# Second-pair sums of y kept in DRAM by accumulating transfers, in a fused attention and two-MLP kernel

## The chip, the cores and the metric

One core of one Trainium2 chip runs the whole program. The metric is device microseconds per execution. The kernel before takes 1046.27 us, the median of 3 runs (1044.96 to 1047.87).

## The reference

Everything is float32. Attention with a soft cap runs over 4 batch rows, 12 heads, 448 positions and head size 64; its result goes through two MLPs.

```
scores = cap * tanh(q @ k.T / sqrt(64) / cap);  x = softmax(scores) @ v     # (4, 12, 448, 64) -> (1792, 768)
h = x @ w_in;  g = h * cos(h);  y = g @ w_out                               # 768 -> 2048 -> 768
a = y @ w1;  b = y @ w2;  out = ((a * b) @ w3) @ w_out2                     # 768 -> 1024 -> 1024 -> 768
```

The w tensors reach the device in double-width words and are converted there. The first MLP's output y is what the change touches.

## The kernel before

**Layout.** Data lie transposed: a tile is 128 features by the 448 positions of one batch row, and the 768 features of y are six such tiles, numbered m = 0 to 5. A product of two float32 operands is three matmuls on high and low parts (`mm3`, L389 to L392), so every product shows as equal numbers of L390, L391 and L392.

**Stages.** Attention for all batch rows comes first, together with the product w3 @ w_out2 (`make_w34`). Then `moe1` makes y. Its first pair of batch rows (b = 0, 1) goes through plain products, unit by unit: a unit is 256 of the 2048 hidden features for one batch row, so a batch row has 8 units. For the second pair (b = 2, 3) both batch rows are worked together in 8 pair steps (`h_step`), each a seven-product scheme of Strassen and Winograd on quarter blocks; sums of x (tiles xS1, xS2, ...) and of w_in (tiles stx, ht, hb) are its operands. Then `moe2` does the second MLP, again by seven products per step, and reads y back from the DRAM scratch `y_d`: for the first pair around its start, for the second pair near its middle (`lefts(1, ...)`).

**y.** For each unit and each m, `y_part` runs six matmuls into a PSUM bank. The first unit of a batch row is copied from the bank to the SBUF tile `y` (ScalarE or VectorE). Each of the 7 later units is added to it by one VectorE instruction that reads bank and tile and writes the tile. After the last unit, SyncE sends the tile to `y_d`. The ring `y_r` has two slots of six tiles; the second MLP takes them over for its own sums (`low`, `high`, shown as y too: `y<-bank,w`, `y<-bank,hs`).

**Order of the work.** A planner in the program (`Plan.schedule`) makes the instruction order of each engine before anything runs. Each operation has a due time, which is a priority and not a start time, and one or more engine options with a cost. The planner is greedy: an engine that is free takes the ready operation that is due first, if ring slots are free. "AD" lets the planner choose ScalarE or VectorE, "PD" GpSimd or VectorE. It models a shared port: an operation that takes the port (all of GpSimd's, and VectorE's with a fourth field in the option) waits for another one that holds it. `pair_due` spaces the pair steps by `pd`; the due times of the second MLP follow from it. All DMAs of the kernel before are issued by SyncE, in planned order, and a DMA at the head of that queue that waits holds up those behind it.

**Pools.** SBUF pools open when others close. Pool lp (tiles rawl, stl) opens when hx closes (the last products of the pair steps), and q2 (tiles rawq, stq) when mp closes (the last y parts). The second MLP converts its weights w1 and w2 in the single slots of rawl and rawq: load, ScalarE L924, GpSimd L930, VectorE L937 and L941, then differences (stq) and high and low parts (xh, xl). The slot rawl first serves the loads of the left operands (A12, S1, S4).

A second copy of the program for caps above 40 sits behind a branch that these inputs don't take.

Of the kernel before, what the change touches and what calls it, by code (L numbers as in the profile page):

```python
# [15 lines left out]
ALU = mybir.AluOpType  # L16
# [4 lines left out]
B, H, S, D = 4, 12, 448, 64  # L21
# [10 lines left out]
BH = B // 2  # L32
# [105 lines left out]
class Plan:  # L138
# [57 lines left out]
    def schedule(self):  # L196
# [10 lines left out]
        free = dict(PE=1.0, ACT=2.0, DVE=3.4, POOL=1.5, SP=1.2, port=0.0)  # L207

        def port(x):
            return x[0] == "POOL" or len(x) > 3  # L210

        free[None] = 0.0
        table, order, t, line = "exp", [], 0.0, 0.0
# [6 lines left out]
        while done < len(self.ops):  # L220
# [6 lines left out]
            for c in cands:  # L227
                o = c[2]
                if o.table and table and o.table != table and o.due > t - SLACK_T and any(
                        x[2].table == table for x in cands):  # L230
                    rest.append(c)
                    continue
                pick = min(o.opts, key=lambda x: max(free[x[0]] - t, free["port"] - t if port(x) else 0.0, 0.0) + wait.get(x[0], 0.0) + x[1] * (PAR.get("w" + (x[0] or ""), 1.0) if o.due < PAR["tw"] else 1.0))
                if pick[0] in idle and port(pick) and free["port"] > t + 1e-9:
                    pick = None
                elif pick[0] not in idle:
                    if len(o.opts) == 1:
                        wait[pick[0]] = wait.get(pick[0], 0.0) + pick[1] * PAR["back"]
                    pick = None
# [9 lines left out]
                for it in o.allocs:  # L249
                    it.ring.queue.remove(it)  # L250
                    it.slot = heapq.heappop(it.ring.free)[1]
                (e, cost, f), two = pick[:3], port(pick)
                if o.table:
                    if table != o.table:
# [49 lines left out]
    ql=6, qs=3,  # L304
    hsw=27,
    wb=(20.0, 81.0), we=(81.5, 150.5), e1=2.6, e2=15.1, e3=20.0,
    m0=163.0, ua=14, pa=19.6, pu=14.75, pd=27.4,
    wlead=3.1,


# [7 lines left out]
    m0=222.0, ua=13, pa=19.15, pu=14.2, nt=9, nph=3,  # L318
# [22 lines left out]
def program(  # L341
# [15 lines left out]
    PE, ACT, DVE, POOL, SP = nc.tensor, nc.scalar, nc.vector, nc.gpsimd, nc.sync  # L357
    G = dict(PAR, **GENERAL) if general else PAR
    plan = Plan()
# [4 lines left out]
    def copy(due, dst, src, n, on, psum=False):  # L364
        opts = {
            "A": ("ACT", (0.051 if psum else 0.094) + n / 1200, lambda: ACT.copy(dst(), src())),  # L366
            "D": ("DVE", 0.068 + n / (960 if psum else 1920), lambda: DVE.tensor_copy(dst(), src()))  # L367
            + (() if psum else (True,)),
            "P": ("POOL", 0.16 + n / 1200,
                  lambda: POOL.tensor_scalar(dst(), src(), 1.0, 0.0, op0=ALU.mult, op1=ALU.add)),  # L370
        }
        plan.op(due, [opts[e] for e in on], r=[src], w=[dst])

    def tt(due, dst, a, b, n, op, on="D", psum=False):
        opts = {
            "D": ("DVE", 0.068 + n / 960, lambda: DVE.tensor_tensor(dst(), a(), b(), op=op))  # L376
            + (() if psum else (True,)),
            "P": ("POOL", 0.158 + n / 480, lambda: POOL.tensor_tensor(dst(), a(), b(), op=op)),  # L378
        }
        plan.op(due, [opts[e] for e in on], r=[a, b], w=[dst])  # L380
# [4 lines left out]
    def dma(due, dst, src, r=(), w=(), kb=115, write=False):  # L385
        plan.op(due, [("SP", 0.66, lambda: SP.dma_start(dst(), src()))], r=r, w=w,
                kb=kb)

    def mm3(out, wh, wl, xh, xl, first, last, on=False):  # L389
        PE.matmul(out, wh, xh, start=first, stop=False, skip_group_check=on)  # L390
        PE.matmul(out, wh, xl, start=False, stop=False, skip_group_check=on)  # L391
        PE.matmul(out, wl, xh, start=False, stop=last, skip_group_check=on)  # L392
# [60 lines left out]
    psum = pools["psum"].pool  # L453
# [24 lines left out]
    y_d = Scratch("dram", [B, KD, P, S], "y_d")  # L478
# [537 lines left out]
    def pair_due(n):  # L1016
        d = G["pd"]
        return unit_due(2 * NP) + (n - 0.26 * (n > 1)) * d

    def unit_due(u):  # L1020
        return G["m0"] + min(u, G["ua"]) * G["pa"] + max(u - G["ua"], 0) * G["pu"]
# [33 lines left out]
    def moe1(raw_r, x_r):  # L1055
# [14 lines left out]
        of = {b: [u for u, x in enumerate(units) if x[1] == b] for b in range(B)}  # L1070
# [58 lines left out]
        def y_part(u, m, due):  # L1129
            g, b = units[u]  # L1130
            gh, gl = g_t[u]
            if u == of[b][0] and m == 0:
                yacc[b] = y_r.new()
            acc = hy_r.ref()
            ws = [w_t["o", g, c] for c in range(2)]

            def f():
                for c in range(2):
                    mm3(acc()[:, :S], ws[c][0]()[:, m * P:(m + 1) * P], ws[c][1]()[:, m * P:(m + 1) * P],
                        gh()[:, c, :], gl()[:, c, :], c == 0, c == 1)  # L1140

            plan.op(due, [("PE", 6 * MM, f)], r=[gh, gl, *ws[0], *ws[1]], w=[acc])
            ya = yacc[b].at(m, lambda t: t[:, m, :])
            if u == of[b][0]:
                copy(due + 1, ya, acc[:, :S], S, "AD", psum=True)
            else:
                tt(due + 1, ya, acc[:, :S], ya, S, ALU.add, psum=True)
            if u == of[b][-1]:
                z = y_d.at((b, m), lambda d: d[b, m])
                dma(due + 3, z, ya, r=[ya], w=[z], kb=230, write=True)  # L1150

# [137 lines left out]
        for u, (g, b) in enumerate(units[:2 * NP]):  # L1289
            u0 = unit_due(u)  # L1290
            pu = unit_due(u + 1) - u0
            if b == groups[g][1][0]:
                weights(g, u0 - G["wlead"])
            for c in range(2):
                wi = w_t["i", g, c]
                hp = hy_r.ref()
                for kp in range(3):
                    due = u0 + (c * 3 + kp) * pu / 6
                    ks = (2 * kp, 2 * kp + 1)

                    plan.op(due, [("PE", 6 * MM, mm_h(hp, wi, ks, xh[b], xl[b]))],
                            r=[*wi, *(z.at(k) for k in ks for z in (xh[b], xl[b]))], w=[hp])
                    if u >= 2:
                        y_part(u - 2, 3 * c + kp, due + pu / 12)
                chain(u, c, hp[:, :S], u0 + (c + 1) * pu / 2)
        half = 36 * MM * 1.02

        def y_pair(n):
            u, after = 2 * NP + 2 * n, pair_due(n + 2) if n + 2 <= NP else pair_due(NP) + 2 * half
            for m in range(KD):  # L1310
                y_part(u, m, after - half + (m + 0.5) * half / KD)
            for m in range(KD * (n + 1 < NP)):
                y_part(u + 1, m, after + (m + 0.5) * half / KD)
# [3 lines left out]
        for n in range(NP):  # L1317
            u, u0, u1 = 2 * NP + 2 * n, pair_due(n), pair_due(n + 1)
# [296 lines left out]
```

## Time and profile before

| | |
|---|---|
| median of 3 runs | 1046.27 us |
| profiled execution | 1047.94 us, span 1046.1 us |
| TensorE (PE) busy | 1022.7 us, 98% |
| VectorE (DVE) busy | 917.8 us, 88% |
| ScalarE (ACT) busy | 566.5 us, 54% |
| GpSimd (POOL) busy | 242.7 us, 23% |
| DMA engines | 50.7% of the span, all from hardware queues |

Busy time is a mean over stages with different limits, so the stages are read one by one. A matmul shows as about 0.36 us but the next one starts 0.20 us after it; a busy share of 100% on PE therefore says little, and the number of matmuls in a window against its length divided by 0.20 us says more. SPq is SyncE's queue, which issues the DMAs. An idle time in brackets is the wait before that instruction and what ended it.

### The profile page before, as it was taken

Reading aid. Unit: us, or ns where it says so; the run is one execution under the profiler, and the core shown is the slowest. Engines: PE = TensorE matmul, PEld = TensorE weight load, DVE = VectorE, ACT = ScalarE, POOL = GpSimd, SP = SyncE. Lnnn points to the kernel's source line nnn. Section 1 sums busy time; section 2 is a strip of 40 time slices with the busy share of each in tenths; the row PEclk is TensorE's granted clock in tenths of the full one; section 3 lists DMA queues with packets and bytes.
Section 4 is the critical chain, followed back from the end, with each engine's and each line's share of the span. In section 5 each row is a group of like instructions: output and inputs, shape, how many; then the busy total and the mean of one; then the engine's idle time right before and its main releaser. Section 6 shows DMA issues by size and latency. Waiting matters only on the chain.

```text
span 1046.1 us, 15415 instructions
## 1 busy us (share of the span) xinstructions
PE 1022.7 (98%) x5560; PEld 872.6 (83%) x5560; DVE 917.8 (88%) x1388; ACT 566.5 (54%) x780; POOL 242.7 (23%) x191
## 2 busy tenths in 40 slices
PE   7999999989999999999999999999999999999997
PEld 2577777768888877897999999999888999999997
DVE  6899999989999999999999889899799888767642
ACT  6779777978687767635564333443334346212121
POOL 4353220212444231225103223211122100000000
PEclk9999999999999999999999999999999999999999
DMA  7666886766665545653545211228455557211132
GB/s 255 203 195 191 232 249 172 224 185 208 208 193 191 182 146 178 194 187 108 191 148 167 95 57 53 103 84 286 154 193 171 166 182 242 79 63 61 61 112 87
DMA packets 82839, 168.84 MB, mean 161 GB/s; under 512 B 19650, under 2 KB 55874, under 8 KB 82754
## 3 DMA queue, kind: packets, MB, share of 16 engines
q1 hardware_dynamic: 82754, 167.78, 50.7%
q8 instruction: 45, 0.74, 0.3%
q14 instruction: 40, 0.33, 0.1%
HBM read 128.94 MB, written 38.62 MB: 160 GB/s over the span
## 4 chain that ended last, share of the span: by engine, by line
PE 46%; DVE 5%; DMA 0%; issue 0%; POOL 0%; ACT 0%; SPq 0%; DVEq 0%; POOLq 0%; ACTq 0%
PE bank L390 16%; PE bank L392 15%; PE bank L391 15%; DVE xl L376 1%; DVE stl L937 1%; DVE y L376 1%; DVE stl L941 1%; DMA rawq<-in_w 0%; DVE stq L376 0%; DVE w34h L367 0%; DVE w34l L376 0%; DVE rawx L376 0%; DVE hs L376 0%; DVE wol L376 0%; DVE g L376 0%
## 5 line engine op out<-in xcount | busy, mean ns | idle before, releaser
L390 PE MATMUL bank<-g,woh 128*128 128x448 f32 x384 | 140.8, 367 | 2.8 <-DVE zs L367 2.8
L392 PE MATMUL bank<-g,wol 128*128 128x448 f32 x384 | 139.8, 364 | 0.0
L391 PE MATMUL bank<-g,woh 128*128 128x448 f32 x384 | 139.3, 363 | 0.0
L672 ACT ACTIVATE double<-double,ts 112x896 f32<-112x896 f32 x96 | 93.8, 982 | 28.9 <-PE double L658 20.3
L376 DVE TENSOR_TENSOR y<-bank,y 128x448 f32<-128x448 f32 x168 | 101.3, 614 | 8.3 <-PE bank L392 8.1
L390 PE MATMUL bank<-xh,wih 128*128 128x448 f32 x264 | 97.1, 368 | 1.9 <-ACT xh L366 1.3
L672 ACT ACTIVATE p<-double,pac 112x896 f32<-112x896 f32 x96 | 96.4, 1013 | 3.1 <-PE bank L706 1.8
L391 PE MATMUL bank<-xl,wih 128*128 128x448 f32 x264 | 96.2, 365 | 1.2 <-POOL xl L378 1.2
L392 PE MATMUL bank<-xh,wil 128*128 128x448 f32 x264 | 96.5, 365 | 0.0
L366 ACT COPY hs<-bank 128x448 f32<-128x448 f32 x72 | 38.2, 531 | 97.3 <-PE bank L392 97.3
L390 PEld LDWEIGHTS bank<-g,woh 128*128 128x128 f32 x384 | 72.3, 188 | 13.9 <-DVE zs L367 3.1
L701 PE MATMUL bank<-p,v 112*32 112x448 f32 x768 | 78.9, 550 | 0.0
L392 PEld LDWEIGHTS bank<-g,wol 128*128 128x128 f32 x384 | 72.5, 189 | 5.3
L391 PEld LDWEIGHTS bank<-g,woh 128*128 128x128 f32 x384 | 72.2, 188 | 4.8
L392 PE MATMUL bank<-ab,w34l 128*128 128x448 f32 x192 | 69.6, 363 | 0.6 <-DVE w34l L376 0.6
L390 PE MATMUL bank<-ab,w34h 128*128 128x448 f32 x192 | 69.7, 363 | 0.0
L391 PE MATMUL bank<-ab,w34h 128*128 128x448 f32 x192 | 69.3, 361 | 0.0
L376 DVE TENSOR_TENSOR p<-p 112x448 f32<-112x448 f32 x79 | 60.3, 765 | 2.5 <-ACT p L672 2.3
L930 POOL TENSOR_SCALAR wx<-rawc 128x768 f32<-128x768 f32 x29 | 39.8, 1373 | 95.1 <-ACT rawc L924 60.5
L701 PEld LDWEIGHTS bank<-p,v 112*32 112x32 f32 x768 | 22.5, 110 | 44.7 <-issue 40.3
L657 PE MATMUL double<-qh,ks 128*112 128x448 f32 x160 | 58.6, 367 | 0.0
L658 PE MATMUL double<-ql,ks 128*112 128x448 f32 x160 | 58.3, 365 | 0.0
(312 smaller groups left out, 2700.1 us busy)
## 6 DMA issues: line engine op xcount, KB each, us to landing
rawc<-in_w_out SPq DMA_DIRECT2D x16, 768.0 KB, 5.1
stq<-w_d SPq DMA_DIRECT2D x32, 384.0 KB, 3.5
rawc<-in_w_in SPq DMA_DIRECT2D x13, 768.0 KB, 5.2
qr<-in_q SPq DMA_DIRECT2D x41, 224.0 KB, 4.1
kr<-in_k SPq DMA_DIRECT2D x41, 224.0 KB, 4.6
raw<-in_w3T SPq DMA_DIRECT2D x16, 512.0 KB, 5.0
stl<-w_d SPq DMA_DIRECT2D x18, 384.0 KB, 3.5
raw<-in_w_out SPq DMA_DIRECT2D x8, 768.0 KB, 5.4
```

Source lines behind the costliest of these rows:

```text
L366: "A": ("ACT", (0.051 if psum else 0.094) + n / 1200, lambda: ACT.copy(dst(), src())),
L376: "D": ("DVE", 0.068 + n / 960, lambda: DVE.tensor_tensor(dst(), a(), b(), op=op))
L390: PE.matmul(out, wh, xh, start=first, stop=False, skip_group_check=on)
L391: PE.matmul(out, wh, xl, start=False, stop=False, skip_group_check=on)
L392: PE.matmul(out, wl, xh, start=False, stop=last, skip_group_check=on)
L657: PE.matmul(o, w, qh(), start=True, stop=False)
L658: PE.matmul(o, w, ql(), start=False, stop=True)
L672: lambda f=f, x=x, o=o: ACT.activation(o(), s(), f, scale=x[:CP]))],
L701: PE.matmul(pv()[q * Q:(q + 1) * Q, :S], w()[:, j, c, d:d + Q], piece(j, c), **flags)
L930: lambda: POOL.tensor_scalar(x(), h_().bitcast(F32), 0.0, 1.0, op0=ALU.mult, op1=ALU.mult)),
L937: DVE.scalar_tensor_tensor(xi, h_(), 3, xi, op0=ALU.logical_shift_left, op1=ALU.bitwise_or)
L941: DVE.scalar_tensor_tensor(xi, l_(), 29, xi, op0=ALU.logical_shift_right, op1=ALU.bitwise_or)
```

## The change

For b = 2 and 3 every unit is copied from the bank to the SBUF tile, by ScalarE or VectorE, the later units too. The first unit's tile is written to `y_d` by SyncE at once. Each later unit's tile is added to what lies in `y_d` by a DMA that GpSimd issues (`accum_op=ALU.add`). The tile is copied over again one unit later. In the planner such a DMA costs GpSimd 1.2 us and doesn't take the port, so `port` now reads the option's fourth field. `pd` goes from 27.4 to 26.5. The first pair (b = 0, 1) stays as it was.

```diff
         def port(x):
-            return x[0] == "POOL" or len(x) > 3
+            return x[3] if len(x) > 3 else x[0] == "POOL"
...
-    m0=163.0, ua=14, pa=19.6, pu=14.75, pd=27.4,
+    m0=163.0, ua=14, pa=19.6, pu=14.75, pd=26.5,
...
             if u == of[b][0]:
                 copy(due + 1, ya, acc[:, :S], S, "AD", psum=True)
+            elif b >= BH:
+                copy(due + 1, ya, acc[:, :S], S, "AD", psum=True)
             else:
                 tt(due + 1, ya, acc[:, :S], ya, S, ALU.add, psum=True)
-            if u == of[b][-1]:
+            if b >= BH:
+                z = y_d.at((b, m), lambda d: d[b, m])
+                if u == of[b][0]:
+                    dma(due + 3, z, ya, r=[ya], w=[z], kb=230, write=True)
+                else:
+                    plan.op(due + 7, [("POOL", 1.2, lambda: POOL.dma_start(z(), ya(), accum_op=ALU.add), False)], r=[ya], w=[z], kb=230)
+            elif u == of[b][-1]:
                 z = y_d.at((b, m), lambda d: d[b, m])
                 dma(due + 3, z, ya, r=[ya], w=[z], kb=230, write=True)
```

## Rows read from the trace of the kernel before

**Rows 1.** Windows by stage: length, busy us (x instructions) per engine, clock, DMA, GB/s.
```profile
476.00:513.00 37.00, 33.84 (x158) 30.13 (x158) 36.47 (x56) 17.59 (x31) 15.29 (x11) 0.95 0.41 132
513.00:718.80 205.80, 205.80 (x1030) 192.89 (x1031) 192.95 (x294) 92.27 (x141) 52.04 (x42) 1.00 0.36 120
718.80:1039.70 320.90, 319.09 (x1585) 296.23 (x1583) 243.27 (x381) 103.20 (x170) 24.42 (x22) 1.00 0.41 138
700.00:725.00 25.00, 25.00 (x127) 23.43 (x126) 23.91 (x45) 8.05 (x15) 4.64 (x3) 1.00 0.87 290
742.00:806.00 64.00, 62.19 (x303) 55.94 (x303) 60.72 (x86) 25.02 (x37) 14.37 (x10) 1.00 0.56 191
```

**Rows 2.** Timeline of PE: start, length, instruction, idle time before it and its releaser.
```profile
492.53 0.47 PE L390 MATMUL bank<-xh,wih 128*128 128x448 f32 x1 [1.34 <-ACT xh L366]
494.25 0.66 PE L391 MATMUL bank<-xl,wih 128*128 128x448 f32 x1 [1.24 <-POOL xl L378]
512.87 0.47 PE L390 MATMUL bank<-xh,wih 128*128 128x448 f32 x1 [0.55 <-DVE hs L376]
...
748.45 0.47 PE L392 MATMUL bank<-yA11h,xl 128*128 128x448 f32 x1 [0.22 <-DVE xl L376]
750.86 0.47 PE L390 MATMUL bank<-yA12h,xh 128*128 128x448 f32 x1 [0.72 <-DVE y L376]
805.61 0.47 PE L392 MATMUL bank<-ab,w34l 128*128 128x448 f32 x1 [0.59 <-DVE w34l L376]
```

**Rows 3.** Tile y, 513 to 721 us: count, ns min/median/max, first and last start.
```profile
L376 DVE TENSOR_TENSOR y<-bank,y x87: 602/616/624, 514.1 to 719.7; 128x448 f32<-128x448 f32 x87
L366 ACT COPY y<-bank x12: 512/533/537, 529.4 to 546.2; 128x448 f32<-128x448 f32 x12
```

**Rows 4.** Groups of instructions of GpSimd, 513 to 721 us.
```profile
L378 POOL TENSOR_TENSOR stx<-stx,stx 128x384 f32<-128x384 f32 x12 | 16.3, 1359 | 74.3 <-DVE ht L376 54.7 <-DMA stx<-wi_d 15.8 <-DVE stx L941 2.4
```

**Rows 5.** Timelines of VectorE and GpSimd: two equal instructions apiece.
```profile
561.27 1.35 DVE L1158 TENSOR_SCALAR w<-hs 128x448 f32<-128x448 f32 x1
...
579.32 0.39 DVE L1158 TENSOR_SCALAR w<-hs 128x448 f32<-128x448 f32 x1
...
757.98 0.88 POOL L930 TENSOR_SCALAR stl<-rawq 128x768 f32<-128x768 f32 x1 [4.16 <-ACT rawq L924]
765.64 4.33 POOL L930 TENSOR_SCALAR stl<-rawl 128x768 f32<-128x768 f32 x1 [6.78 <-ACT rawl L924]
```

**Rows 6.** DMA issues, 540 to 725 us: KB each, median us to landing.
```profile
y_d<-y SPq DMA_DIRECT2D x12, 224.0 KB, 5.0
```

**Rows 7.** Timelines of SPq, DVE and POOL at the second MLP's start, in order of time.
```profile
707.64 3.58 SPq L386 DMA_DIRECT2D y_d<-y  x4
717.30 2.92 SPq L386 DMA_DIRECT2D y_d<-y  x4
720.27 1.77 SPq L386 DMA_DIRECT2D rawl<-ls_d  x3
722.67 0.62 DVE L376 TENSOR_TENSOR y<-bank,w 128x448 f32<-128x448 f32 x1 [0.98 <-PE bank L392]
730.76 1.70 DVE L376 TENSOR_TENSOR yS4l<-rawl,yS4h 128x448 fp32r<-128x448 f32 x3
732.49 0.33 SPq L386 DMA_DIRECT2D rawl<-in_w  x1
739.80 1.31 POOL L930 TENSOR_SCALAR stl<-rawl 128x768 f32<-128x768 f32 x1 [30.17 <-ACT rawl L924]
742.96 0.95 DVE L937 SCALAR_TENSOR_TENSOR stl<-rawl,stl 128x768 uint32<-128x768 uint32 x1
```

**Rows 8.** Windows of 5 us around that start; columns as in Rows 1.
```profile
715.00:720.00 5.00, 5.00 (x27) 4.68 (x25) 4.93 (x11) 0.78 (x2) 0.00 (x0) 1.00 1.01 325
725.00:730.00 5.00, 5.00 (x26) 4.69 (x25) 4.03 (x8) 2.55 (x5) 0.00 (x0) 1.00 0.54 210
730.00:735.00 5.00, 5.00 (x26) 4.67 (x25) 3.58 (x7) 1.26 (x3) 0.00 (x0) 1.00 0.55 149
735.00:740.00 5.00, 5.00 (x26) 4.69 (x26) 2.83 (x5) 2.71 (x4) 0.20 (x1) 1.00 0.21 87
```

## The prediction

> **What bounds the kernel now.** I read the busy shares first, then windows by stage, then the timeline of PE with its releasers. The shares name two candidates, PE (98%) and DVE (88%). The windows decide between them stage by stage. From 513.0 to 718.8 us, the eight pair steps, PE starts 1030 matmuls in 205.8 us, 0.1998 us each, and is busy throughout [rows 1]. The timeline shows no wait of PE in that stage. I take 0.1998 us as the pace of an unhindered PE, and matmuls times pace against a window's length as the time lost in it. From 718.8 to 1039.7 us there are 1585 matmuls, 316.7 us of work in 320.9: 4.2 us lost. Of this, 742 to 806 us loses 3.5 us (303 matmuls, 60.5 us of work in 64.0), and there DVE is 95% busy [rows 1]. From 476 to 513 us, the change to the second pair, 158 matmuls are 31.6 us of work in 37.0: 5.4 us lost, in part because the granted clock falls to 0.95 of full speed (a part of the stretch at 1.2 GHz) after the first waits; DVE is 99% busy. The waits behind these losses end in results of DVE, or of POOL and ACT at 492 to 494 us [rows 2]. So PE's count sets the time, and only these two places, 9.6 us together, can be given back; what happens before 476 us comes before the first operation that the change moves by more than a due time.
>
> **Removed: 84 additions on DVE.** Two batch rows, seven later units, six tiles: 84 of the 87 `y<-bank,y` in the window, at 0.616 us [rows 3], 51.7 us of DVE's 193.0. They lie wholly beside a PE that never waits, so the stage itself gets no shorter by them.
>
> **Added: 84 copies.** ACT's copy of a bank to y takes 0.533 us at the median [rows 3]; 44.8 us if ACT takes all, beside the 92.3 it has in 205.8 [rows 1]. That fits, at 67%. The 12 copies of the first units all went to ACT, so I expect ACT to take most of the 84. Cost to the end: nothing, as long as banks come free in time; there are eight, each part fills one in 1.2 us, and a copy is no slower than the addition. If DVE took them all, nothing would be won or lost: its price per copy is close to that of the addition.
>
> **Added: 84 accumulating DMAs on POOL.** The trace has no DMA of POOL's. The bounds for POOL's time in one are the issue of a plain DMA by SyncE, 0.33 us, and POOL's longest instruction, 4.33 us [rows 5, 7]. The nearest row is an ordinary POOL instruction, 1.36 us mean [rows 4]; I take that. 84 of them are 114 us, with 52.0 us of present work 166 of 205.8 [rows 1]: POOL goes from 25% to 81% and holds. The limit is (205.8 - 52.0) / 84 = 1.83 us each. The bytes, 84 transfers of 224 KB, are 18.8 MB, and twice that if a read of what lies in `y_d` is counted: 92 to 183 GB/s on top of 120 in this stage, which has moved 290 for 25 us [rows 1]. The waits that these DMAs bring: POOL's later work (operand differences stx, hb for the next pair step) queues behind one that waits for its copy; it is made some us ahead of use, and GpSimd idles 54.7 us of the stage in waits for DVE's ht alone [rows 4]. And a copy must wait until the unit before has left its tile. That is 135 matmuls, 27 us, earlier within the stage and 14.4 us for the last units, against some 0.5 + 1.4 + 5.0 us of copy, issue and landing [rows 3, 4, 6]; I cost it at nothing.
>
> **Removed: 12 late writes on SyncE,** in exchange for 12 early ones in a quiet stretch. Groups of four held SyncE's queue for 3.58 us and 2.92 us, waiting for the additions, with the loads of the second MLP's operands behind them [rows 7].
>
> **Where the relief can arrive.** The second MLP's first conversion chain starts with the load of w into rawl at 732.49 us. That load waits for the slot, which yS4l frees at 732.4; its own loads were issued at 720.27, behind four writes of y. ScalarE and POOL follow (739.80), then DVE at 742.96 [rows 7]; from there DVE has no slack, and PE loses its first time at 748 to 751 [rows 2]. Ahead of it, from 700 to 720, DVE was full and carried 18 of the additions, one every 1.2 us, 18 times 0.616 or 11.1 us. From 725 to 740 DVE idled 0.97 + 1.42 + 2.17 = 4.6 us, waiting for this chain to deliver [rows 8]. With additions and writes gone, the chain can start earlier and that idle time can be filled: up to 4.6 us of DVE's work goes ahead of 742, against 4.2 us lost. What holds it back: the DMA engines are 100% busy from 715 to 720 [rows 8], 18 accumulating transfers fall into 700 to 722 instead of 12 writes, and the slots are single. I take two thirds, 2.8 us. Bounds: all 4.2 us gained, or the loss of the second rival.
>
> **`pd` from 27.4 to 26.5.** PE needs 27.0 us a pair, so no start is held by it; it moves priorities within a pair step by up to 0.9 us. At 512.87 PE waits 0.55 us for DVE's hs, whose due time now comes 0.8 us sooner [rows 2]. I take 0.8 us gained, this wait and a bit of its wake. A new order can as well cost as gain; I bound it by the 5.4 us lost there, either way.
>
> **The sum.** 0 in the pair steps, -2.8, -0.8: -3.6 us. The profiled execution took 1047.94 us (span 1046.1), 1.67 us above the median of the runs, 1046.27; it would take 1044.3, and the median 1042.7 us.
>
> **Rival one: no difference.** The additions were hidden behind PE, and what replaces them is hidden too. The 3.5 us at 742 to 806 stay, because DVE's work there (conversions, differences, low parts) doesn't change and its slots don't let it run ahead; the load into rawl stays late because the accumulating transfers take the DMA engines at the time it needs them. For it: 95% of DVE in that window is without additions of units. Against it: the idle DVE just before. Time 1046.3, from 1043.2 to 1049.4. It holds also where the planner gives most copies to DVE.
>
> **Rival two: POOL is late at the hand-over.** The last four units, 24 tiles, leave PE at 1.2 us apiece. If a DMA costs POOL c us, the thirteenth (b = 2, m = 0 of the last unit) is 13 (c - 1.2) late. Its part ends at 718.8 - 11 x 1.2 = 705.6; with 0.5 of copy, 1.2 and 5.0 to landing [rows 3, 6] it is done at 712.3. The second MLP's first sum (722.67 on DVE) writes into that slot [rows 7], 10.4 us later. So it decides from c = 2.0 us; beyond, that sum stands at the head of DVE's queue with everything behind it. At twice the planner's price, c = 2.4, 5.2 us: 1051.5 us. For it: DVE and POOL hold each other up in this trace, one DVE form takes 0.39 us alone and 1.35 us beside POOL, and one POOL form 0.88 and 4.33 us [rows 5]. Against it: POOL is nearly free from 709 to 740 (a wait of 30.17 us [rows 7]), so a late queue has room to empty, and DVE's additions from PSUM are fewer.
>
> The Trainium skill (SBUF — State Buffer, section "SBUF: two separate sides") speaks for rival two: it says that a DMA from GpSimd stalls while VectorE runs an instruction that takes the port pair the two share, because GpSimd can't write descriptors then, and gives some 620 ns alone and 3100 ns beside such a copy. With 3.1 us the same sum would give 13 x 1.9 - 10.4 = 14.3 us, an estimate of 1060.6 us; that the two engines hold each other up agrees with the rows just named, that a DMA of POOL's does so no row here shows.
>
> **How the numbers follow.** A run differs from another of this kernel by up to 0.3%, 3.1 us here; less than that is no difference that can be told. Forecast 0.42, rival one 0.34, rival two 0.24. The forecast's own range is 1038.5 (4.2 us and 3.5 of the 5.4) to 1043.1. The range for all reaches to rival two's 1051.5: 1038.5 to 1051.5. Chances: faster 0.42, same 0.34, slower 0.24.
>
> **What would show it.** Right: 0.20 us per matmul and no wait of PE from 513 to 718 us; ACT with some 80 copies of y in that stage; POOL's DMAs at 1 to 1.8 us each; the load of w into rawl, counted from the last y part (now 13.7 us behind it), some us earlier; over 310 matmuls in the 64 us from 23 us behind that part. Wrong: the load no earlier, or 303 matmuls again (rival one); DVE's first sum of the second MLP waiting for a DMA of y (rival two); copies waiting for such DMAs inside the pair steps; a loss above 5.4 us at 476 to 513 (the new order).

## The result and the profile after

The changed kernel takes 1055.76 us at the median (1053.41 to 1061.16), beside 1047.07 us for the kernel before on the same chip: ratio 1.0086, 95% interval 1.0057 to 1.0114. It is 8.7 us slower (interval 6.0 to 11.9). Forecast were 1042.7 us and a range of 1038.5 to 1051.5; the time lies above both, on the side of the second rival.

The profiled execution, the lowest of the runs, took 1053.41 us with a span of 1051.6 us, 5.5 us longer than the span of before. The two lowest runs (1053.41 and 1053.64 us) had a mean granted clock of 0.994 to 0.995 and the other four 0.990 to 0.991, so the trace shows some 5.5 of the 8.7 us, and where the rest goes no trace here shows. Where the 5.5 us are lost, the windows by stage show (columns as in [rows 1]). The kernel after:

```profile
476.00:513.00 37.00, 33.70 (x158) 30.40 (x157) 36.43 (x57) 17.57 (x31) 14.86 (x10) 0.95 0.42 131
513.00:718.60 205.60, 205.60 (x1030) 192.71 (x1029) 164.95 (x255) 121.84 (x203) 84.67 (x86) 1.00 0.92 205
718.60:743.00 24.40, 22.79 (x109) 19.70 (x108) 15.72 (x28) 6.99 (x13) 10.14 (x11) 1.00 1.05 231
743.00:806.00 63.00, 59.97 (x290) 53.28 (x289) 58.25 (x85) 25.41 (x38) 13.38 (x10) 1.00 0.56 185
806.00:860.00 54.00, 53.41 (x267) 49.65 (x266) 47.02 (x74) 20.65 (x35) 6.01 (x5) 1.00 0.51 162
```

The kernel before, the last three of these windows, which [rows 1] cuts otherwise or lacks:

```profile
718.60:743.00 24.40, 24.40 (x123) 22.86 (x122) 18.53 (x33) 7.65 (x13) 2.53 (x2) 1.00 0.53 185
743.00:806.00 63.00, 61.19 (x298) 55.00 (x298) 60.02 (x85) 25.02 (x37) 14.03 (x9) 1.00 0.57 194
806.00:860.00 54.00, 54.00 (x271) 50.55 (x270) 47.21 (x79) 23.28 (x41) 3.75 (x4) 1.00 0.53 171
```

The pair steps are as fast as they were: 1030 matmuls in 205.6 us, though the share of the DMA engines rose from 0.36 [rows 1] to 0.92 there. The stretch from 476 to 513 us is unchanged too. The loss begins where the pair steps end: 109 matmuls in place of 123, then 290 in place of 298. These 22 matmuls are 4.4 us at 0.2 us each, and the window after it lacks four more, 0.8 us: together 5.2 of the 5.5 us.

What happens there stands in the timelines of the kernel after (start, length, engine, instruction, and in brackets the idle time before it and its releaser; I put GpSimd first, then ScalarE, VectorE, SyncE's queue and TensorE):

```profile
716.89 0.87 POOL L1155 DMA_DIRECT2D y_d<-y  x1 [0.96 <-issue]
...
741.80 0.87 POOL L1155 DMA_DIRECT2D y_d<-y  x1 [3.63 <-issue]
...
721.94 0.53 ACT L366 COPY y<-bank 128x448 f32<-128x448 f32 x1 [2.45 <-DMA y_d<-y]
...
724.74 0.62 DVE L376 TENSOR_TENSOR y<-bank,w 128x448 f32<-128x448 f32 x1 [7.29 <-DMA y_d<-y]
...
739.42 0.33 SPq L386 DMA_DIRECT2D rawl<-in_w  x1
...
722.96 0.48 PE L390 MATMUL bank<-yS2h,xh 128*128 128x448 f32 x1 [0.93 <-ACT w L366]
752.18 0.47 PE L390 MATMUL bank<-yA11h,xh 128*128 128x448 f32 x1 [0.68 <-ACT xh L366]
754.05 0.47 PE L392 MATMUL bank<-yA11h,xl 128*128 128x448 f32 x1 [1.20 <-DVE xl L376]
```

The last 24 transfers of GpSimd start from 691.04 to 741.80 us: 50.8 / 23 = 2.2 us each, while the parts come at 1.2 us each. The thirteenth of them is the one at 716.89; in the chain of work that ended last its time to landing is the next piece:

```profile
716.89 7.73 DMA y_d<-y
```

That ends at 724.62, and 0.12 us later VectorE starts its first sum of the second MLP, for which it has stood still 7.29 us. Most of this wait is not the transfer's. The product that fills the sum's bank ends at 722.0 us (its last matmul starts at 721.67 and takes 0.36), so the landing adds 2.6 us; with plain transfers in the same order, shown below, VectorE stands still 4.84 us at this place for the bank alone. The sum starts 2.1 us later than in [rows 7], and casts that stood ahead of it in the kernel before, and had to come before the next loads, are behind it. The load of w into rawl follows the last part of y by 21.4 us (739.42 after a last matmul that starts at 718.07), where it was 13.9 counted in the same way (the prediction's 13.7 counts from 718.8).

Page and tile view of the kernel after, the queues (packets, MB, share of 16 engines) and the instructions on tile y that answer to [rows 3]:

```profile
q1 hardware_dynamic: 82754, 167.78, 51.2%
q0 software_dynamic: 12096, 19.27, 12.5%
```

```profile
L366 ACT COPY y<-bank x85: 512/534/540, 528.9 to 719.0; 128x448 f32<-128x448 f32 x85
L367 DVE COPY y<-bank x10: 616/624/624, 554.1 to 701.7; 128x448 f32<-128x448 f32 x10
```

The second queue is GpSimd's: 0.125 x 16 x 1051.6 / 84 = 25.0 us of engine time per transfer, 1.57 us if all 16 work at it, in 144 packets. ScalarE took most copies, as expected.

### The profile page after: what moved, and what is told of

Its sections match the earlier page's. It is cut to its first block, busy times and chain, and to the rows that moved or that the text cites. A ratio compares the mean times of both kernels' runs of the same rounds, so it can differ in the third digit from the quotient of the medians.

```text
span 1051.6 us, 15642 instructions
## 1 busy us (share of the span) xinstructions
PE 1023.8 (97%) x5560; PEld 872.1 (83%) x5560; DVE 889.3 (85%) x1353; ACT 597.3 (57%) x844; POOL 280.4 (27%) x246
## 3 DMA queue, kind: packets, MB, share of 16 engines
q0 software_dynamic: 12096, 19.27, 12.5%
## 4 chain that ended last, share of the span: by engine, by line
PE 77%; DVE 8%; issue 5%; DMA 4%; POOL 3%; ACT 2%; SPq 0%; POOLq 0%; DVEq 0%; ACTq 0%
PE bank L390 22%; PE bank L392 21%; PE bank L391 21%; PE bank L701 6%; PE double L657 2%; PE double L658 2%; POOL y_d L1155 2%; PE double L647 1%; PE bank L706 1%; DVE xl L376 1%; DMA y_d<-y 1%; DMA kr<-in_k 1%; DMA rawc<-in_w_in 1%; DVE p L376 1%; DMA rawl<-in_w 1%
## 5 line engine op out<-in xcount | busy, mean ns | idle before, releaser
L1155 POOL DMA_DIRECT2D y_d<-y x84 | 77.0, 927 | 89.2 <-ACT y L366 35.5
L366 ACT COPY y<-bank 128x448 f32<-128x448 f32 x95 | 50.3, 532 | 47.9 <-PE bank L392 40.5
L930 POOL TENSOR_SCALAR wx<-rawc 128x768 f32<-128x768 f32 x29 | 36.7, 1265 | 97.2 <-ACT rawc L924 67.3
L376 DVE TENSOR_TENSOR hs<-bank,hs 128x448 f32<-128x448 f32 x40 | 24.8, 620 | 42.9 <-PE bank L392 42.7
```

The lines of the kernel that those rows point to most:

```text
L930: lambda: POOL.tensor_scalar(x(), h_().bitcast(F32), 0.0, 1.0, op0=ALU.mult, op1=ALU.mult)),
L1155: plan.op(due + 7, [("POOL", 1.2, lambda: POOL.dma_start(z(), ya(), accum_op=ALU.add), False)], r=[ya], w=[z], kb=230)
```

## The experiments

Times are medians; ratios are to the kernel before on the same chip. Diffs are against the changed kernel unless another is named.

### The parts by themselves

The constant alone, against the kernel before:

```
-    m0=163.0, ua=14, pa=19.6, pu=14.75, pd=27.4,
+    m0=163.0, ua=14, pa=19.6, pu=14.75, pd=26.5,
```

> The kernel before with the pair spacing at 26.5 alone; the additions stay on VectorE. Theory A (the accumulating transfers make the change slow): within 3 us of the kernel before, about 1047. Rival B (the new order costs the time): about 1053 to 1056, with PE losing some 10 us around the start of the second MLP.

1047.34 us, 1.0003 (0.9992 to 1.0013). The constant alone gives and takes nothing that can be told.

The relief of VectorE alone: copies, no transfers between, the last unit written by SyncE (no sums over the units).

```
-            if b >= BH:
...
-                    plan.op(due + 7, [("POOL", 1.2, lambda: POOL.dma_start(...
-            elif u == of[b][-1]:
+            if u == of[b][-1]:
```

> The 84 additions are taken from VectorE and copies of ScalarE or VectorE stand in their place, but there are no transfers in between; only the last unit of each row is written, by SyncE, as in the kernel before (the sums over the units are left out). Forecast on record: the relief of VectorE at the entry of the second MLP is worth 2.8 us and the other constant 0.8 us, which would be 1043.4 us, ratio 0.9965. Theory now (the pair steps are bound by TensorE and the entry by the order of VectorE's work and by loads): ratio 0.999 to 1.001, with the first load of w into rawl no sooner behind the last part of y than in the kernel before (13.7 us).

1045.84 us, 0.9979 (0.9969 to 0.9990): by the ratio 2.2 us faster, by the medians 1.2. The theory that it is worth nothing falls. Window and queue of that run:

```profile
743.00:806.00 63.00, 62.04 (x308) 57.03 (x307) 61.61 (x87) 25.41 (x38) 14.05 (x12) 1.00 0.59 195
```

```profile
724.60 0.33 SPq L386 DMA_DIRECT2D rawl<-in_w  x1
```

The load comes 5.8 us behind the last part (718.82) and the window holds 308 matmuls in place of 298. That is the step as it was forecast, with the 12 late writes of SyncE still in place.

The same with the old constant (`pd=27.4`):

> As the relief alone (copies, no transfers in between; the sums over the units are left out), with the old constant of the planner's due times (27.4 in place of 26.5). If the 2.2 us below the kernel before come from VectorE's 84 shorter instructions and the transfers that they no longer bring late: ratio 0.997 to 0.999. If they come from the constant together with the relief: 0.9995 to 1.001.

1043.88 us, 0.9968 (0.9956 to 0.9980). The relief stays with the old constant; whether this is better than with the new one, the two intervals don't tell.

### What the transfers cost

Plain transfers (each unit overwrites the one before; the adding is left out):

```
-   ... lambda: POOL.dma_start(z(), ya(), accum_op=ALU.add), False)], ...
+   ... lambda: POOL.dma_start(z(), ya()), False)], ...
```

> The changed kernel with GpSimd's 84 transfers as plain writes to DRAM; left out is the adding, so y holds its last unit alone. The order is the same. Theory A1 (the adding makes the transfers slow, and GpSimd's queue waits for them): GpSimd issues one per 1.2 us in the last four units, the first sum of the second MLP waits for none, the time is 1046 to 1049. Rival A2 (GpSimd's descriptor writing is slow beside VectorE): the interval stays near 2.4 us, the wait of 7.3 us and the time near 1055 stay.

1048.87 us, 1.0014 (1.0002 to 1.0026). The planned order is that of the changed kernel, so about 7 us of the loss are the adding's. Queue and timeline of this run:

```profile
q0 software_dynamic: 5376, 19.27, 4.8%
```

```profile
721.49 0.62 DVE L376 TENSOR_TENSOR y<-bank,w 128x448 f32<-128x448 f32 x1 [4.84 <-PE bank L392]
...
736.24 0.33 SPq L386 DMA_DIRECT2D rawl<-in_w  x1
```

The same 19.27 MB in 64 packets a transfer and 0.048 x 16 x 1047.1 / 84 = 9.6 us of engine time. GpSimd takes 0.54 us for one in place of 0.87, keeps to 1.2 us, and VectorE waits for no y. But the load into rawl is 18.8 us behind the last part: the relief has not arrived.

Two plain transfers per unit, the second into a scratch area (`z2`):

```
-   ... lambda: POOL.dma_start(z(), ya(), accum_op=ALU.add), False)], r=[ya], w=[z], kb=230)
+   ... lambda: (POOL.dma_start(z(), ya()), POOL.dma_start(z2(), ya())), False)], r=[ya], w=[z, z2], kb=230)
```

> Each accumulating transfer of GpSimd becomes two plain ones of the same tile, the second into a scratch area that nobody reads (the adding is left out). In the run of plain writes one took 9.6 us of DMA engine time in 64 packets and 0.54 us of GpSimd; two make 19.2 us, 128 packets and 1.1 us, against 25.0 us, 144 packets and 0.87 us of one accumulating transfer. Theory (the load on the 16 DMA engines and the descriptors that GpSimd has to fit in at the hand-over cost the time, whatever the packets do): most of the way back to the changed kernel, ratio to the kernel before 1.005 to 1.009, GpSimd's last 24 units 1.5 to 2.2 us apart, and VectorE's first sum of the second MLP waits again for a transfer of y. Rival (it is the adding itself, the reading back from DRAM and the order of the additions, that costs): as with one plain write, ratio 1.000 to 1.003, units 1.2 us apart.

1050.89 us, 1.0035 (1.0022 to 1.0047): between the two theories. The engine time is 0.098 x 16 x 1049.2 / 84 = 19.6 us a unit, GpSimd's last 24 units run at some 1.8 us each, yet VectorE's first sum does not wait for y (at 722.52 it has waited for a bank). So without any adding a second plain transfer costs some 2 us more than one; whether by the load on the DMA engines or by GpSimd's second issue, this run doesn't separate. 25.0 us with adding cost 8.7 us, 19.6 us without 3.7.

Room for GpSimd's descriptors, 1408 and 512 bytes:

```
-    nc = _bacc.Bacc("TRN2", target_bir_lowering=False, num_devices=1, dynamic_dma_scratch_size=1024)
+    nc = _bacc.Bacc("TRN2", target_bir_lowering=False, num_devices=1, dynamic_dma_scratch_size=1408)
```

> The changed kernel with 1408 instead of 1024 bytes of a partition for GpSimd's descriptors. If room for descriptors holds GpSimd back (rival A3), the interval between its transfers falls from 2.4 us to about 1.8 and the time by some us, to about 1050. If the adding itself is the limit (A1) nothing changes: 1054 to 1056, the interval near 2.4 us.

> The changed kernel with 512 bytes for GpSimd's descriptors, half. Rival A3 (room for descriptors is the limit): the interval grows to some 4 to 5 us, PE waits inside the pair steps, 1080 us or more. A1: only few transfers are ever in flight, so 1054 to 1060.

With 1408 bytes 1056.72 us, 1.0098 (1.0077 to 1.0118); with 512 bytes 1239.29 us, 1.1844 (1.1824 to 1.1863). The room sets the pace of GpSimd when the queue is full: 4.2, 2.2 and 1.65 us a transfer at 512, 1024 and 1408 bytes, the last near the 1.57 us of all 16 DMA engines. At 512 TensorE waits inside the pair steps, up to 28.0 us at a time, as rival A3 expected; that only few transfers are in flight and little changes was wrong. At 1408 VectorE no longer waits for y (0.72 us for the bank at 724.76), but the time stays. DMA issues of the kernel after from 680 to 745 us (KB each, us to landing):

```profile
stl<-ls_d SPq DMA_DIRECT2D x6, 224.0 KB, 8.6
rawl<-ls_d SPq DMA_DIRECT2D x6, 224.0 KB, 6.7
stl<-w_d SPq DMA_DIRECT2D x2, 384.0 KB, 5.8
```

of the run with 1408 bytes:

```profile
stl<-ls_d SPq DMA_DIRECT2D x6, 224.0 KB, 11.6
rawl<-ls_d SPq DMA_DIRECT2D x6, 224.0 KB, 13.0
stl<-w_d SPq DMA_DIRECT2D x2, 384.0 KB, 12.1
```

and of the kernel before:

```profile
stl<-ls_d SPq DMA_DIRECT2D x6, 224.0 KB, 4.8
rawl<-ls_d SPq DMA_DIRECT2D x6, 224.0 KB, 4.9
stl<-w_d SPq DMA_DIRECT2D x2, 384.0 KB, 5.9
```

With more room the loads are late in place of y. The 24 transfers of the last two units of both rows are 24 x 1.57 = 38 us of all 16 engines, in the 29 us in which their parts come, and the second MLP's loads want the same engines. That agrees with the Trainium skill (DMA: Bandwidth & Descriptors, section "Issuing engines are not separate DMA queues"), by which transfers of all issuing engines run on the same 16 DMA engines.

### Fewer transfers

Two units summed in SBUF before each transfer, 36 in place of 84:

```
-            elif b >= BH:
+            elif b >= BH and of[b].index(u) % 2 == 0:
...
-            if b >= BH:
+            if b >= BH and of[b].index(u) % 2 == 0:
+                pass
+            elif b >= BH:
...
-                if u == of[b][0]:
+                if u == of[b][1]:
```

> Every second unit is again summed in SBUF by VectorE, so that there are 36 accumulating transfers in place of 84 and 12 in place of 24 behind the last two units of the pair. Theory (24 transfers of 25.0 us engine time each within 29 us at the hand-over are what costs): the last 12 keep their pace with the parts, VectorE's first sum of the second MLP no longer waits for y, loads land about as in the kernel before; ratio to the kernel before 1.000 to 1.003, about 1047 to 1050 us. Rival (the transfers of the whole pair, not those of its end, cost the time, in proportion to their number): 36/84 of the loss stays, ratio 1.004.

1047.12 us, 0.9996 (0.9988 to 1.0005): the loss is gone, while the load into rawl is no earlier than in the kernel before (14.6 us behind the last part). Only the last two units of each row together, 72 transfers, 12 at the end (in the same way, with `u != of[b][-1]` and `u == of[b][-2]`):

> As the changed kernel, but for each of the second pair's two batch rows the last unit is added in SBUF to the one before it, and one transfer takes both: 72 accumulating transfers in place of 84, and 12 in place of 24 behind the last two units; the earlier units keep theirs. Theory (the loss is at the hand-over alone): ratio 1.000 to 1.004, PE's share of the loss between the last part of y and the second MLP gone, no wait of VectorE for y. Rival (the loss goes with the number of transfers over the whole pair): 72/84 of it stays, ratio 1.007.

1045.91 us, 0.9986 (0.9974 to 0.9999): 10 us below the changed kernel by leaving out 12 of its 84 transfers. Its windows:

```profile
513.00:718.60 205.60, 205.60 (x1030) 192.74 (x1029) 170.16 (x265) 121.79 (x203) 79.05 (x79) 1.00 0.88 200
718.60:743.00 24.40, 24.40 (x124) 22.83 (x123) 17.55 (x26) 7.22 (x13) 7.84 (x9) 1.00 0.76 158
743.00:806.00 63.00, 61.59 (x305) 56.53 (x304) 60.62 (x83) 25.90 (x39) 16.40 (x14) 1.00 0.58 201
```

The DMA share in the pair steps is nearly that of the changed kernel (0.88 against 0.92), and nothing is lost: the number over the whole pair doesn't count. At the end two things changed, 12 transfers in place of 24 and, as the planner counts fewer bytes, an earlier load: it is 7.8 us behind the last part. The next runs show that the number alone does not decide. The same kernel with the old constant:

> As the run with the last two units in one transfer (0.9986), with the old constant of the due times (27.4). The relief alone gave 0.9979 with the new and 0.9968 with the old constant. If the constant carries over: 0.997 to 0.998; if the order around the transfers decides instead: anything from 0.998 to 1.003.

1046.26 us, 0.9993 (0.9984 to 1.0002). The gain hoped for from the old constant is not there; the two intervals overlap.

The last three units together, 60 transfers, again 12 at the end:

> As the run with the last two units in one transfer, with the last three of each row: 60 accumulating transfers, none between those of the units up to the fourth and the last 12. Theory (what is left of the loss are the transfers in the last 29 us, 12 in either run, and the relief of VectorE is worth up to 2.2 us): 0.998 to 0.9995, not measurably below the run with the last two units (0.9986). Rival (each transfer over the pair costs a share): lower than that run by about 0.001 to 0.0015, 0.997 to 0.998.

1056.84 us, 1.0087 (1.0073 to 1.0101): both expectations failed. The timeline of this run:

```profile
733.61 0.86 POOL L1157 DMA_DIRECT2D y_d<-y  x1 [0.48 <-issue]
734.17 1.32 POOL L378 TENSOR_TENSOR stq<-stl,stq 128x384 f32<-128x384 f32 x1
...
735.52 0.56 DVE L376 TENSOR_TENSOR stq<-stl,stq 128x384 f32<-128x384 f32 x1 [6.61 <-POOL stq L378]
...
737.54 0.74 PE L390 MATMUL bank<-wih,xh 128*128 128x448 f32 x1 [6.15 <-DVE hs L376]
```

The planner gave a sum of weights to GpSimd, behind the twelve transfers. GpSimd reaches it at 734.17, VectorE stands still 6.6 us for it, TensorE 6.1. This is the late queue of GpSimd again, with another victim. Behind the wait TensorE is also slower for a while; the window that follows:

```profile
738.00:742.00 4.00, 4.00 (x14) 3.58 (x14) 0.66 (x2) 0.20 (x1) 0.00 (x0) 0.62 0.34 100
```

In these 4 us it starts 14 matmuls where the unhindered pace is 20, at a granted clock of 0.62: most of the window at the lower of its two levels, 1.2 GHz, after one matmul in the 4 us before. So such a wait costs more than its own length; the same shows in the runs with no bytes counted and with 1408 bytes (0.79 and 0.93 from 718.6 to 743 us).

### The order that the planner writes

The planner counts 230 KB for each transfer and writes the loads later for it. With nothing counted (`kb=0`), once with the adding and once with plain transfers (no adding):

```
-   ... r=[ya], w=[z], kb=230)
+   ... r=[ya], w=[z], kb=0)
```

> The same 84 accumulating transfers, but the planner that writes the order out counts them with no bytes (0 in place of 230 KB), so that it puts the loads of the second MLP as early as if the DMA engines were free: VectorE's first sum of the second MLP then stands behind all casts of yS1 to yS4, as in the kernel with the relief alone. Theory (the DMA engines and GpSimd's own queue are overfull for some 25 us at the hand-over): the transfers cost what they cost, ratio to the kernel before 1.005 to 1.011. Rival (the planner's charge delays the loads in the order written out, and that is most of the loss): ratio 0.998 to 1.002.

> As the run of plain writes (no adding), with the planner counting no bytes for them. Plain writes with the charge gave 1.0014, no transfers at all 0.9979. If the 3.5 thousandths between them are the order that the charge writes (the load of w into rawl 18.8 us behind the last part of y against about 7): 0.998 to 0.9995, with that load within 10 us of the last part. If they are the transfers themselves: 1.001 to 1.002.

Plain: 1045.55 us, 0.9990 (0.9978 to 1.0003); the load is 4.2 us behind the last part (721.34 after 717.17), and 743 to 806 us holds 316 matmuls. So the plain run had lost its relief mostly, it seems, through the order that the count writes (1.0014 to 0.9990; the intervals just touch). With the adding: 1064.57 us, 1.0168 (1.0154 to 1.0182), slower than either expectation. Timeline of that run:

```profile
742.35 1.23 POOL L378 TENSOR_TENSOR stq<-stl,stq 128x384 f32<-128x384 f32 x1
...
743.61 2.05 DVE L367 CAST xh<-stq 128x768 fp32r<-128x768 f32 x1 [12.97 <-POOL stq L378]
...
728.82 0.74 PE L390 MATMUL bank<-yS2h,xh 128*128 128x448 f32 x1 [7.55 <-DVE w L367]
747.24 0.74 PE L390 MATMUL bank<-wih,xh 128*128 128x448 f32 x1 [6.42 <-DVE hs L376]
```

The same sum of weights, behind all 24 transfers, and VectorE waits 13.0 us. So the count that costs the plain transfers something saves the adding ones some 8 us; with it, in the changed kernel, these sums of weights all stand on VectorE. The test of what stands on GpSimd: the first sums, casts and remainders of the second MLP kept off GpSimd, in both kernels.

```
-    def halves(due, z, src, n):
+    def halves(due, z, src, n, late=False):
-        copy(due, z[0], src, n, "ADP")
-        lo(due + 0.5, z[1], src, z[0], n)
+        copy(due, z[0], src, n, "AD" if late else "ADP")
+        lo(due + 0.5, z[1], src, z[0], n, "D" if late else "PD")
...
+            late = p == 0 and fc < 3
...
-            tt(due - 3, t1, b12, b11, HALF, ALU.subtract, "PD")
+            tt(due - 3, t1, b12, b11, HALF, ALU.subtract, "D" if late else "PD")
```

> As the run with the last three units in one transfer, but the sums, casts and remainders of the second MLP's first weights and stored operands may not go to GpSimd. In that run the 384-column weight sum stood on GpSimd behind the last of the twelve y transfers, at 734.17, with VectorE waiting 6.6 us and TensorE 6.1 us for it. Theory (GpSimd runs late on its transfers, by 1.8 us or more per transfer, and what stands behind them on GpSimd, or needs their tile, pays): without it the ratio falls from 1.0087 to 0.997 to 1.001. Rival (it is the loads beside the transfers that land late, and another wait takes the place): 1.005 to 1.009.

> The 84 accumulating transfers counted with no bytes, and GpSimd kept free of the same work. In the run before it the weight sum stood on GpSimd behind the last transfer, at 742.35, and VectorE waited 13.0 us for it, TensorE 7.6 and 6.8 us at weight loads. Theory: 8 us or more of the 17.6 us above the kernel before go; since 24 transfers at about 2.2 us each still end some 20 us behind the last copy and their y slots are wanted, 1.002 to 1.008. Rival (the DMA engines, not GpSimd's queue): 1.012 or more.

Three units: 1052.85 us, 1.0060 (1.0047 to 1.0074), in place of 1.0087. Some 3 us are gone, but the ratio is above the theory's 0.997 to 1.001 and inside the rival's 1.005 to 1.009: another wait has taken the place. Uncharged: 1057.15 us, 1.0092 (1.0077 to 1.0108), in place of 1.0168. That is the 8 us expected, yet the ratio lies between the theory's and the rival's. What waits in the second:

```profile
723.91 0.53 ACT L366 COPY y<-bank 128x448 f32<-128x448 f32 x1 [0.68 <-DMA y_d<-y]
...
744.27 0.87 POOL L1155 DMA_DIRECT2D y_d<-y  x1 [1.10 <-issue]
744.84 1.21 POOL L930 TENSOR_SCALAR stl<-rawl 128x768 f32<-128x768 f32 x1
...
746.08 1.62 DVE L937 SCALAR_TENSOR_TENSOR stl<-rawl,stl 128x768 uint32<-128x768 uint32 x1 [4.58 <-POOL stl L930]
...
748.29 0.74 PE L391 MATMUL bank<-ab,w34h 128*128 128x448 f32 x1 [5.86 <-DVE ab L376]
```

A conversion that the planner gave to GpSimd stands behind the last transfer, VectorE waits 4.6 us for it, and the operand that TensorE needs is next in VectorE's queue. Removing one victim uncovers the next. In the run with three units the transfers end at 729 us and no work on GpSimd waits for them any more; what waits is this (ScalarE, GpSimd, TensorE):

```profile
739.24 0.93 ACT L924 ACTIVATE rawl<-rawl 128x768 f32<-128x768 f32 x1 [3.75 <-DMA rawl<-in_w]
742.19 0.56 POOL L370 TENSOR_SCALAR ab<-y 128x448 fp32r<-128x448 f32 x1 [12.15 <-PE bank L392]
742.72 0.87 POOL L930 TENSOR_SCALAR stl<-rawl 128x768 f32<-128x768 f32 x1
748.28 0.48 PE L390 MATMUL bank<-yA11h,xh 128*128 128x448 f32 x1 [2.57 <-ACT xh L366]
```

The load into rawl is 18.5 us behind the last part (735.00), behind casts of VectorE that the order puts after a second sum. That sum starts at 731.36, 0.09 us after the end of the product that fills its bank, which points to that bank and not to a transfer. The conversion L930 then starts some 2.5 us after ScalarE has done (740.17): a cast `ab` that the planner gave to GpSimd stands ahead of it and, by the chain of waits, follows a product of VectorE that ends at 742.01. VectorE's steps L937 and L941 come behind that, and TensorE waits 2.6 us for their result. So the order that the edit wrote is part of the 6 us left; how they divide stays open.

The last two units together, old constant, GpSimd kept free in the same way:

> As the run beside it (last two units in one transfer, old constant), with GpSimd kept free of the second MLP's first sums, casts and remainders. If GpSimd's queue is what is left: 0.996 to 0.9975, the version below both kernels. If VectorE's added work costs what the queue gave: 0.998 to 1.0.

1047.27 us, 1.0002 (0.9993 to 1.0011), beside 0.9993: taking the work off GpSimd gives nothing back. It also moved the load into rawl from 7.8 to 12.9 us behind the last part, so this run does not tell what GpSimd's queue costs with half the transfers at the end.

## Why the prediction was wrong

**The pair steps** were right: no wait of TensorE, 84 additions gone from VectorE without a gain in the stage, ScalarE with most copies, DMA engines at 0.92 and still hidden.

**The accumulating DMAs, costed at nothing, are the step that failed,** and with it the wait for a tile to leave, put at nothing as well. The price of 1.36 us was put on GpSimd's time, and that was even too high: 0.87 us. What sets the pace is how fast a transfer clears the descriptors' room and the 16 DMA engines, and neither was priced. In the pair steps a unit's 12 transfers have the whole step, and nothing shows. At the end 24 come within 29 us. There c, taken from start to start, was 2.2 us. In the sum "0.5 + 1.4 + 5.0" of copy, issue and landing the queue is missing: the thirteenth landed 7.73 us after a start that was 10.8 us late (716.89 in place of 705.6 + 0.5). The bytes were counted twice in the prediction, for the read, but in an average over the stage; no count was made for the last 29 us, where the loads are. Nor do GB/s tell the load: the stage went from 120 to 205, less than the 290 that the prediction set beside it, while the share of the DMA engines went from 0.36 to 0.92. (The bytes are 19.27 MB and not 18.8; nothing hangs on it.)

**Rival two named the place and the first wait:** the thirteenth transfer, VectorE's first sum, everything behind it. Its sum by c = 2.2 gives 13 x 1.0 - 10.4 = 2.6 us; that sum of VectorE started 2.1 us later than before, so the size was right too. But 8.7 us were lost, and with more room this wait went and the time stayed, with late loads in its place. The loads, the order that the planner wrote and the clock behind waits were in no sum. The reason drawn for it was not borne out: GpSimd's instruction took 0.87 us, and plain transfers went out every 1.2 us (0.54 us each) beside a VectorE that is busy four fifths of the stage. The Trainium skill's 3100 ns (SBUF — State Buffer, section "SBUF: two separate sides") is seen in no run here, where GpSimd's longest instruction for a transfer of y took 1.6 us in the pair steps of the changed kernel; nor do these runs isolate such a hold.

**The relief at the second MLP's entry, -2.8 us, was right in sign and near in size:** by the ratios 2.2 us alone, 3.3 us with the old constant. In the changed kernel its step "the chain can start earlier" failed: the load came 21.4 us behind the last part in place of 13.9. Plain transfers lost it too (18.8), and with their bytes left uncounted by the planner they kept it (4.2). So rival one's sign, a load no earlier, came as well, but plain transfers on the DMA engines did not bring it; the count did, which the prediction did not look at. The adding ones lost it through the queue as well.

**The constant, -0.8 us,** is not seen: 1.0003 (0.9992 to 1.0013). The wait of 0.55 us at 512.87 [rows 2], which it was to remove, is gone in the trace of the constant alone, but stands in that of the plain transfers with the same constant (0.64 us at 511.29).

**The chances** gave 0.24 to the slower side. The bounds for c (0.33 to 4.33 us) contained the deciding 2.0 well inside, but c was taken for the time of GpSimd's instruction. That took 0.87 us and was no limit; the start-to-start time of a full queue is another quantity, and no row of the kernel before could show it.

## What to carry to other kernels

Price a transfer three times, in its issuing engine, in the DMA engines and in the tile that it holds, and take the sum over the busiest stretch and not over the stage: what is free for 200 us can be overfull for the last 29. When work moves to an engine's queue, list what is already planned on that engine after it; here a sum of weights and a conversion paid, once the first wait was gone. And a gain may be there and be lost by another part of the same change: with half the transfers at the end 8.7 us lost became 0.9986 of the time before, about the bound of what can be told. Where a planner writes the order, each edit also writes a new one: another arrangement with as many transfers at the end came to 1.0087.

## What the runs showed of the hardware

An accumulating transfer of 224 KB took the DMA engines 25.0 us of engine time in 144 packets, a plain one 9.6 us in 64, and GpSimd 0.87 us against 0.54. With 512, 1024 and 1408 bytes of room for descriptors GpSimd's full queue ran at 4.2, 2.2 and 1.65 us a transfer. With 1408 bytes, where the share of the DMA engines stands at 1.06 from 718.6 to 743 us, loads of SyncE's queue took up to 13.0 us to land (median of six) in place of 4.9. In a wait of TensorE of 6.15 us that ended at 737.54 and behind it the granted clock was 0.52 (734 to 738 us) and 0.62 (738 to 742).
